# An edge tile, four and four PSUM banks, a shifted weight plan, and a weight decoding that VectorE shares with ScalarE and GpSimd

## The chip, the cores and the metric

One Trainium2 chip, one core. The time is that of the program on the device in microseconds; lower is better. The profile is that of one execution of its own.

## What is computed

Linear attention, then a mixture of four experts weighted by given probabilities, then a feed-forward layer with a sigmoid GELU:

```python
# q, k, v: (4, 8, 576, 64)
q_s = softmax(q, axis=-1); k_s = softmax(k, axis=2)
x = einsum('bhsd,bhde->bhse', q_s, einsum('bhsd,bhse->bhde', k_s, v))
x = x.transpose(0, 2, 1, 3).reshape(2304, 512)
p = domain_probs / domain_probs.sum(-1)                       # (2304, 4)
out = sum(p[:, e:e+1] * (relu(x @ w1[e]) @ w2[e]) for e in range(4))   # w1 (4, 512, 1024)
h = out @ w_in                                                # (512, 2048)
return (h * sigmoid(1.702 * h)) @ w_out                       # (2048, 512)
```

`w_in` and `w_out` come as float64, that is as pairs of 32-bit words; everything else is float32.

## The kernel before

Every float32 matrix is split into a high and a low part (`h`, `l`), each of a type that TensorE reads in one pass, and a product is three matmuls (high-high, high-low, low-high). The first layer of each of the two networks is done as a 2x2 block product with seven products in place of eight (Strassen's form, as Winograd ordered it): the weights give seven blocks (`a11, a12, a22, s1..s4`), the tokens seven "forms" (`b11, b21, b22, t1..t4`). One product is six matmuls (L836).

Work goes in units: a unit is 256 columns of the hidden width, 16 for the experts and 8 for the feed-forward layer. Tokens are in three groups of 2x512, 2x256 and 2x384 columns (groups 0, 1, 2). Pass 0 of each network runs all units over group 0; pass 1 runs all units over groups 1 and 2, one step each. A step (`step`) has five stages, in an order written out by hand (STAGES): products m1 to m7 into the PSUM tiles `px`, `py`, `pz`; ScalarE copies (`p1c`, `u2c`, `u3c`) and VectorE additions (`p1a`, `u2a`, `u3a`, L866) that combine them; ScalarE's relu or GELU into `h_hi` (`ra` to `rd`, L879) and VectorE's `h_lo` (`la` to `ld`, L885, L889). A step finishes the one before it (a dash marks its operations). TILES and REST, in stages 4 and 1, are the second layer: for every 128 tokens six matmuls of 512 columns into a PSUM tile `po` (L952), which VectorE adds to the accumulator `acc` (L964 for the experts, L973 for the feed-forward layer).

PSUM has eight banks: the pool `psc` has five (tag "c": `px`, `py`, `pz`), the pool `pso` three (tag "o": `po`, and the attention's transposes and products `pm`, `pb`, `pk`, `t`, `px` of L531). A tile takes the bank of its pool that has been free longest, and its first writer waits for that bank's last reader.

At the end of each stage `prepare` makes the next unit's weight parts by the plans TWO (two steps a unit) or ONE (pass 0): sums on GpSimd (L762), the high part on ScalarE (L768), the low part on GpSimd (L774). Then the background is pumped: `pump` advances generators, `pumps[0]` times a stage on average. They are the attention of the later batches in the first half of pass 0 (rate 2), and in pass 1 of the experts `decode_all` (rate 1.4), which turns 32 tiles of 128x512 float64 weights into float32. A tile takes four pumps there (`decode`): lines 803 and 804; 808 and 811; 815 and 818; 820 and 823. Only line 823 is GpSimd's, the others VectorE's. The load of the next tile (`w64`, line 796, two buffers) is issued on SP's queue after a tile's third pump, and the store of its result (line 824) after the second pump of the next tile. Each engine works through its instructions in the order of the program.

The forms of groups 0 and 2 lie in the pools `xp0` and `xq0`, opened from the right-hand end of SBUF (4 KB a tile and partition, the last ending 32 bytes short of the end); those of group 1 lie in `xp1`, on the left.

Of the kernel before, what the change touches and what calls it, by code (L numbers as in the profile page):

```python
# [8 lines left out]
F32 = mybir.dt.float32  # L9
# [6 lines left out]
ALU = mybir.AluOpType  # L16
# [6 lines left out]
def tile_linear_attention_moe_gelu(  # L23
# [56 lines left out]
    evp = ctx.enter_context(tc.tile_pool(name="evp", bufs=7))  # L80
    xop = ctx.enter_context(tc.tile_pool(name="xop", bufs=2))
    dram = ctx.enter_context(tc.tile_pool(name="dram", bufs=1, space=DRAM))
    psc = ctx.enter_context(tc.tile_pool(name="psc", bufs=5, space=PSUM))
    pso = ctx.enter_context(tc.tile_pool(name="pso", bufs=3, space=PSUM))

    ident = const.tile([P, P], F32, name="ident")
    ones = const.tile([P, SP], F32, name="ones")
# [10 lines left out]
    def open_pool(name, **kw):  # L98
        pools[name] = tc.tile_pool(name=name, reuse_waits="tile", **kw)
        pools[name, "p"] = pools[name].__enter__()  # L100

    def close_pool(name):
        pools.pop(name).__exit__(None, None, None)
        pools.pop((name, "p"))

    wi32 = dram.tile([DM, FF], F32, name="wi32")
    wo32 = dram.tile([FF, DM], F32, name="wo32")

# [19 lines left out]
    def probs_ops():  # L128

        y = {}

        def pr_(_):
            n = evp.tile([SP, B, NCH, E], F32, tag="ev", name="prn")
            sh = evp.tile([SP, 3 * SP], F32, tag="ev", name="shift")
            sm = evp.tile([SP, B * NCH], F32, tag="ev", name="prs")
            y.update(sh=sh, sm=sm, f=n.rearrange("p b c e -> p (b c) e"))  # L140
            S_.dma_start(
                out=n.rearrange("p b c e -> p b (c e)"),
                in_=probs.rearrange("(b p c) e -> p b (c e)", b=B, c=NCH),
            )
# [12 lines left out]
        def pp(_):  # L157
            f, sh = y["f"], y["sh"]
            ps = y["ps"] = pso.tile([P, NT // P, E], F32, tag="o", name="pr_ps")
            by_tile = ps.rearrange("p (x t) e -> p x t e", t=3)  # L160
            by_group = f.rearrange("p (x g) e -> p x g e", g=4)
            for t in range(3):
                first = [(0, *divmod(t * P, SP))]
                first += [((g * SP) - t * P, g, 0) for g in range(4) if t * P < g * SP < (t + 1) * P]
                for x, (o, g, p0) in enumerate(first):
                    T.matmul(
                        by_tile[:, :, t, :], sh[:, SP + p0 - o : SP + p0 - o + P], by_group[:, :, g, :],
                        start=(x == 0), stop=(x == len(first) - 1), skip_group_check=True,
                    )

        def pc(_):
            V.tensor_copy(pr, y["ps"])

        return {"pr": pr_, "pn": pn, "pp": pp, "pc": pc}


# [39 lines left out]
    def attend(b, j, pool, bufs, x, small_bufs):  # L216
# [10 lines left out]

        def bank(s, n):
            if n in KBANK[b]:
                return psc.tile(s, F32, tag="c", name=f"{n}_{nm}")  # L230
            return pso.tile(s, F32, tag="o", name=f"{n}_{nm}")

        def qm(_):
            y["qm"] = small([SP, 2 * NCH], "qm")
# [171 lines left out]
    def attend2(b, j, c0, nc_, keys, live):  # L406
# [9 lines left out]
            return pools["attn2", "p"].tile(s, F32, tag=tag or n, bufs=BUFS.get(tag or n, 2), name=f"{n}{nm}")  # L416

        def bk(n, s):
            return pso.tile(s, F32, tag="o", name=f"{n}_{nm}")

        def lq(_):
            y["q"] = t_("q", [SP, 2, nc_, D])
# [226 lines left out]
    def to_x2(i, ti, lt):  # L649

        src = acc[ti]

        def go():
            pt = pso.tile([P, KT, P], F32, tag="o", name=f"pt{ti}")
            for kk in range(KT):
                T.transpose(pt[:, kk, :], src[:, kk * P : (kk + 1) * P], ident)
            o = xop.tile([P, KT * P], F32, tag="xo", name=f"xt{ti}")
            copy(V if stage[1] else A, o, pt.rearrange("p k t -> p (k t)"))
            A.dma_start(out=x_d["ffn", i][:, :, lt * P : (lt + 1) * P], in_=o.rearrange("p (k t) -> p k t", t=P))

        x2.append((stage[0], go))
# [130 lines left out]
    def decode(src, dst, pool, nm):  # L792

        n = src.shape[1]
        w = pool.tile([P, n], I64, tag="w64", name=f"w64{nm}")
        S_.dma_start(out=w, in_=src)
        yield
        w = w.bitcast(I32).rearrange("p (n t) -> p n t", t=2)
        top, low = w[:, :, 1], w[:, :, 0].bitcast(U32)
        s = pool.tile([P, n], I32, tag="ds", name=f"ds{nm}")  # L800
        t = pool.tile([P, n], I32, tag="dt", name=f"dt{nm}")
        o = pool.tile([P, n], F32, tag="do", name=f"do{nm}")
        V.tensor_scalar(out=s, in0=top, scalar1=0x7FF00000, scalar2=None, op0=ALU.bitwise_and)
        V.tensor_scalar(
            out=s, in0=s, scalar1=float(1151 << 20), scalar2=float(896 << 20), op0=ALU.min, op1=ALU.max
        )
        yield
        V.tensor_scalar(
            out=s, in0=s, scalar1=float(896 << 20), scalar2=8.0, op0=ALU.subtract, op1=ALU.mult
        )  # L810
        V.scalar_tensor_tensor(  # L811
            out=s, in0=top, scalar=-(1 << 31), in1=s, op0=ALU.bitwise_and, op1=ALU.bitwise_or
        )
        yield
        V.tensor_scalar(
            out=t, in0=top, scalar1=3, scalar2=0x007FFFF8, op0=ALU.logical_shift_left, op1=ALU.bitwise_and
        )
        V.tensor_tensor(out=t, in0=t, in1=s, op=ALU.bitwise_or)
        yield
        V.scalar_tensor_tensor(  # L820
            out=o, in0=low, scalar=2.0**-52, in1=s.bitcast(F32), op0=ALU.mult, op1=ALU.mult
        )
        G.tensor_tensor(out=o, in0=o, in1=t.bitcast(F32), op=ALU.add)  # L823
        late.append(lambda: S_.dma_start(out=dst, in_=o))
        yield
# [16 lines left out]
    def mm1(g, i, m, ho):  # L842
# [7 lines left out]
        def product(ps, w, t, first):  # L850
            def go(_):
                if first:
                    y[ps] = psc.tile([P, n], F32, tag="c", name=f"{ps}{nm}")
                mm(y[ps], W1[m, w], X[i, t], first, True)

            return go
# [36 lines left out]
        if m < NPLAIN:  # L893
            def half(x, ft, kh):
                def go(_):
                    if kh == 0:
                        y["c" + x] = psc.tile([P, n], F32, tag="c", name=f"c{x}{nm}")
                    b = f"b{kh + 1}{1 + (i == 'R')}"
                    mm(y["c" + x], W1[m, f"a{ft + 1}{kh + 1}"], X[0, b], kh == 0, kh == 1)

                return go

            tile_of = {"a": (0, 0, "ca"), "c": (1, 0, "cc")}
            for x, (ft, *_) in tile_of.items():
# [31 lines left out]
    def mm2(g, i, lt, m, ho):  # L936
# [6 lines left out]
        y = {}  # L943

        def product(_=None):
            y["ps"] = ps = pso.tile([P, DM], F32, tag="o", name=f"po{g}_{ti}")
            n = 0
            for ft in range(FT):
                hh, hl = h_hi[:, ft, s], h_lo[:, ft, s]
                wh, wl = W2[m, ft]  # L950
                for a, b in ((hh, wh), (hh, wl), (hl, wh)):
                    T.matmul(ps, a, b, start=(n == 0), stop=(n == 3 * FT - 1))  # L952
                    n += 1
# [49 lines left out]
        (("s1",), ("a11", "s2"), ("a12",), ("+s2", "s3"), ("s4",)),  # L1003
        ((), ("+s1",), ("+s3",), ("a22",), ("+s4",)),
    )
    ONE = ((("s1", "a11"), ("s2", "a12"), ("+s2", "s3"), ("+s1", "s4", "+s3"), ("a22", "+s4")),)

    def prepare(m, names):
        for x in names:
# [57 lines left out]
    def step(k_, tiles, before):  # L1067
# [77 lines left out]
        a1:s5 c1:s5 St3:b0@V Ht3:b0 y0:s4 a2:s5 ha22:6 la22:6@G y1:s4 z0:s4 ra:s5 Lt3:b0@V la:s5 z1:s4 c2:s5 rc:s5  # L1145
        lc:s5 y2:s4 ha12:6 hs2:6 la12:6@V y3:s4 z2:s4 hs3:6 ls2:6@V z3:s4 ls3:6@V hs1:6 ls1:6@G St4:b0@G
    """
    open_pool("xp0", bufs=2, side="right")
    open_pool("x0", bufs=1)
    open_pool("attn", bufs=1)  # L1150
# [3 lines left out]
    V.memset(warm, 0.0)  # L1154
    small0 = attn.tile([P, 1], F32, name="small0")
    V.memset(small0, 0.0)
    hot = psc.tile([P, P], F32, tag="c", name="hot")

    def keep_warm(n):

# [42 lines left out]
    for x in START.split():  # L1203
# [20 lines left out]
    for layer, g0 in (("moe", LM), ("ffn", 2 * LM + LF)):  # L1224
        ka, kb = at_step[g0 - 4, 0], at_step[g0 - 1, 0]
        if layer == "moe":
            when(ka, 3, drain, lambda: open_pool("xp1", bufs=2))
        when(ka, 3, load_now(layer, 1))
        when(ka, 4, forms_now(layer, 1, OWN))
        when(kb - 1, 4, load_now(layer, 2))  # L1230
        when(kb, 1, forms_now(layer, 2, SHARED, work(1.4, decode_all(tiles)) if layer == "moe" else lambda: None))
    kc = at_step[2 * LM - 1, 2]
    when(kc - 1, 0, drain, load_now("ffn", 0))
    when(kc, 1, forms_now("ffn", 0, SHARED))
# [4 lines left out]
    for y in tiles_at(len(steps) - 1):  # L1239
        for x in mm2(*y):  # L1240
            x()
    for name in ("xp1", "xq0", "xp0"):
        close_pool(name)
    manual.__exit__(None, None, None)

# [25 lines left out]
```

## Time and profile before

| | us |
|---|---|
| median of 3 runs | 1256.05 (1254.97 to 1257.68) |
| profiled execution | 1257.08 |
| its span | 1255.3 |
| TensorE busy | 1217.9 (97%) |
| VectorE busy | 848.0 (68%) |
| ScalarE busy | 464.6 (37%) |
| GpSimd busy | 356.8 (28%) |

The share of busy time is a mean over stretches with different limits. TensorE's matmuls overlap in the records, so that its pace is read from pieces of the chain (so many matmuls in so many us), not from the duration of one. VectorE's instructions overlap by some 0.08 us at their ends. Times in the rows are us from the start of the span.

### The profile page before, as it was taken

Reading aid. Unit: us, or ns where it says so; the run is one execution under the profiler, and the core shown is the slowest. Engines: PE = TensorE matmul, PEld = TensorE weight load, DVE = VectorE, ACT = ScalarE, POOL = GpSimd, SP = SyncE. Lnnn points to the kernel's source line nnn. Section 1 sums busy time; section 2 is a strip of 40 time slices with the busy share of each in tenths; the row PEclk is TensorE's granted clock in tenths of the full one; section 3 lists DMA queues with packets and bytes.
Section 4 is the critical chain, followed back from the end, with each engine's and each line's share of the span. In section 5 each row is a group of like instructions: output and inputs, shape, how many; then the busy total and the mean of one; then the engine's idle time right before and its main releaser. Section 6 shows DMA issues by size and latency. Waiting matters only on the chain.

```text
span 1255.3 us, 17519 instructions
## 1 busy us (share of the span) xinstructions
PE 1217.9 (97%) x6276; PEld 1047.6 (83%) x6276; DVE 848.0 (68%) x1416; ACT 464.6 (37%) x1010; POOL 356.8 (28%) x389
## 2 busy tenths in 40 slices
PE   8999899999999999999999999999999999999998
PEld 8777678777887898888989899998787778999997
DVE  7865777666567758999999855577446665455454
ACT  6534344433434351222222222145645444333332
POOL 5425657454553001111211311025555400000000
PEclk9999899999999999999999999999999999999999
DMA  9875965754566375766556332535664655333333
GB/s 211 261 267 179 313 179 199 215 206 143 203 226 201 110 214 189 213 214 219 202 201 227 129 105 77 191 120 195 225 231 180 206 170 161 109 96 115 117 94 84
DMA packets 134423, 225.86 MB, mean 180 GB/s; under 512 B 30400, under 2 KB 62144, under 8 KB 133696
## 3 DMA queue, kind: packets, MB, share of 16 engines
q1 hardware_dynamic: 124832, 220.02, 54.3%
q10 hardware_dynamic: 9504, 4.72, 1.3%
q8 instruction: 50, 0.82, 0.3%
q14 instruction: 37, 0.30, 0.1%
HBM read 137.40 MB, written 87.29 MB: 179 GB/s over the span
## 4 chain that ended last, share of the span: by engine, by line
PE 71%; DVE 18%; DMA 5%; issue 3%; ACT 2%; POOL 1%; SPq 0%; ACTq 0%; DVEq 0%; POOLq 0%
PE po L952 35%; PE px L836 17%; PE pz L836 7%; PE py L836 5%; DVE acc L964 4%; DVE h_lo L885 3%; DMA w64o<-in_moe_w_out 1%; DMA w64i<-in_moe_w_in 1%; DVE u L866 1%; PE p L378 1%; PE pk L506 1%; DMA k_a<-a 1%; DMA q<-in_q 1%; PE px L358 1%; DVE dso L811 1%
## 5 line engine op out<-in xcount | busy, mean ns | idle before, releaser
L952 PE MATMUL po<-w,h_hi 128*128 128x512 f32 x1728 | 541.7, 395 | 14.2 <-DVE acc L964 8.0
L952 PEld LDWEIGHTS po<-w,h_hi 128*128 128x128 f32 x1728 | 320.8, 189 | 82.3 <-DVE acc L964 9.5
L952 PE MATMUL po<-w,h_lo 128*128 128x512 f32 x864 | 339.3, 393 | 5.2 <-DVE h_lo L885 5.2
L964 DVE SCALAR_TENSOR_TENSOR acc<-po,pr,acc 128x512 f32<-128x512 f32 x270 | 195.2, 746 | 77.6 <-PE po L952 77.3
L952 PEld LDWEIGHTS po<-w,h_lo 128*128 128x128 f32 x864 | 163.3, 189 | 42.3 <-DVE h_lo L885 7.0
L110 ACT COPY u<-px 128x384 f32<-128x384 f32 (+2 forms) x138 | 65.2, 472 | 243.5 <-PE px L836 240.1
L973 DVE TENSOR_TENSOR acc<-po,acc 128x512 f32<-128x512 f32 x126 | 85.9, 689 | 62.2 <-PE po L952 62.0
L774 POOL TENSOR_TENSOR s<-s,s 128x256 fp32r<-128x256 f32 x94 | 77.1, 821 | 140.3 <-ACT s L768 121.1
L866 DVE TENSOR_TENSOR u<-pz,u 128x384 f32<-128x384 f32 (+2 forms) x138 | 75.5, 547 | 58.0 <-ACT u L110 57.3
L787 POOL TENSOR_TENSOR w<-rc,w 128x512 fp32r<-128x512 f32 x46 | 59.8, 1299 | 75.6 <-ACT w L781 56.2
L879 ACT ACTIVATE h_hi<-px 128x256 fp32r<-128x256 f32 (+2 forms) x45 | 21.8, 484 | 152.0 <-PE px L836 151.8
L885 DVE SCALAR_TENSOR_TENSOR h_lo<-u,h_hi 128x256 fp32r<-128x256 f32 (+2 forms) x90 | 62.9, 723 | 14.1 <-ACT h_hi L879 14.1
L774 POOL TENSOR_TENSOR a<-ra,a 128x256 fp32r<-128x256 f32 x69 | 52.1, 757 | 57.6 <-ACT a L768 56.6
L823 POOL TENSOR_TENSOR doi<-doi,dti 128x512 f32<-128x512 f32 x16 | 21.1, 1320 | 155.7 <-DVE doi L820 149.2
L762 POOL TENSOR_TENSOR s<-ra 128x256 f32<-128x256 f32 x48 | 41.1, 857 | 84.2 <-DMA ra<-wi 54.2
L866 DVE TENSOR_TENSOR p<-py,p 128x384 f32<-128x384 f32 (+2 forms) x69 | 37.8, 548 | 37.3 <-PE py L836 32.9
L781 ACT CAST w<-rc 128x512 fp32r<-128x512 f32 x48 | 29.6, 620 | 70.5 <-PE po L952 69.8
L879 ACT ACTIVATE h_hi<-u 128x256 fp32r<-128x256 f32 (+2 forms) x90 | 46.3, 515 | 24.9 <-DVE u L866 24.9
L823 POOL TENSOR_TENSOR doo<-doo,dto 128x512 f32<-128x512 f32 x16 | 21.1, 1320 | 96.8 <-DVE doo L820 83.5
L110 ACT COPY p<-px 128x384 f32<-128x384 f32 (+2 forms) x69 | 32.8, 476 | 39.2 <-PE px L836 38.9
L885 DVE SCALAR_TENSOR_TENSOR h_lo<-px,h_hi 128x256 fp32r<-128x256 f32 (+2 forms) x45 | 24.6, 546 | 31.1 <-ACT h_hi L879 31.1
L768 ACT CAST s<-s 128x256 fp32r<-128x256 f32 x96 | 36.8, 401 | 20.6 <-POOL s L762 15.3
(312 smaller groups left out, 2458.8 us busy)
## 6 DMA issues: line engine op xcount, KB each, us to landing
w<-k_w SPq DMA_DIRECT2D x54, 512.0 KB, 4.5
k_w<-w SPq DMA_DIRECT2D x48, 512.0 KB, 4.9
a<-k_a SPq DMA_DIRECT2D x84, 256.0 KB, 2.8
k_s<-s SPq DMA_DIRECT2D x84, 256.0 KB, 4.5
s<-k_s SPq DMA_DIRECT2D x84, 256.0 KB, 3.3
k_a<-a SPq DMA_DIRECT2D x75, 256.0 KB, 4.9
ra<-in_moe_w SPq DMA_DIRECT2D x19, 512.0 KB, 4.4
rc<-in_moe_w SPq DMA_DIRECT2D x16, 512.0 KB, 5.9
```

Source lines behind the costliest of these rows:

```text
L110: (eng.copy if eng is A else eng.tensor_copy)(o, i)
L762: G.tensor_tensor(out=o, in0=block_w(m, l), in1=block_w(m, r), op=op)
L774: eng.tensor_tensor(out=lo, in0=block_w(m, x), in1=hi.bitcast(F32), op=ALU.subtract)
L787: eng.tensor_tensor(out=lo, in0=raw[m, 1][:, c, :], in1=hi.bitcast(F32), op=ALU.subtract)
L823: G.tensor_tensor(out=o, in0=o, in1=t.bitcast(F32), op=ALU.add)
L836: T.matmul(ps, a[:, kk, :], b[:, kk, :], start=(start and n == 0), stop=(stop and n == 5), skip_group_check=True,)
L866: return lambda _: V.tensor_tensor(out=y[o], in0=y[ps], in1=y[o], op=ALU.add)
L879: A.activation(hi, y[c], AF.Relu)
L885: V.scalar_tensor_tensor(out=lo, in0=y[c], scalar=0.0, in1=hi.bitcast(F32), op0=ALU.max, op1=ALU.subtract)
L952: T.matmul(ps, a, b, start=(n == 0), stop=(n == 3 * FT - 1))
L964: V.scalar_tensor_tensor(out=acc[ti], in0=ps, scalar=pe, in1=acc[ti], op0=ALU.mult, op1=ALU.add)
L973: V.tensor_tensor(out=acc[ti], in0=ps, in1=acc[ti], op=ALU.add)
```

## The change

Five edits:

- A tile of 224 bytes a partition (`edge`) is opened at the right-hand end of SBUF ahead of `xp0` and kept, so that every tile of `xp0` and `xq0` starts 224 bytes lower.
- After the start both PSUM pools are closed and opened again with four banks each.
- In the plan ONE, a12 is made one stage later, and so are the parts of s2 and s3.
- In `decode`, VectorE's steps of lines 808 and 820 go. ScalarE makes `s` (scale 8 and a bias) and, from the low word, `o` (scale 2^-52), both behind line 804; the sign is put in one pump later, in front of the "or" with the mantissa; GpSimd then multiplies `o` by `s` and adds `t`. A tile has four pumps as before.
- The background's rate while decoding is 1.25 and not 1.4.

```diff
+    open_pool("psc", bufs=5, space=PSUM)
+    open_pool("pso", bufs=3, space=PSUM)
...
         V.tensor_scalar(
             out=s, in0=s, scalar1=float(1151 << 20), scalar2=float(896 << 20), op0=ALU.min, op1=ALU.max
         )
-        yield
-        V.tensor_scalar(
-            out=s, in0=s, scalar1=float(896 << 20), scalar2=8.0, op0=ALU.subtract, op1=ALU.mult
-        )
-        V.scalar_tensor_tensor(
-            out=s, in0=top, scalar=-(1 << 31), in1=s, op0=ALU.bitwise_and, op1=ALU.bitwise_or
-        )
+        A.activation(s, s, AF.Copy, bias=-float(896 << 23), scale=8.0)
+        A.activation(o, low, AF.Copy, scale=2.0**-52)
         yield
         V.tensor_scalar(
             out=t, in0=top, scalar1=3, scalar2=0x007FFFF8, op0=ALU.logical_shift_left, op1=ALU.bitwise_and
         )
+        yield
+        V.scalar_tensor_tensor(
+            out=s, in0=top, scalar=-(1 << 31), in1=s, op0=ALU.bitwise_and, op1=ALU.bitwise_or
+        )
         V.tensor_tensor(out=t, in0=t, in1=s, op=ALU.bitwise_or)
         yield
-        V.scalar_tensor_tensor(
-            out=o, in0=low, scalar=2.0**-52, in1=s.bitcast(F32), op0=ALU.mult, op1=ALU.mult
-        )
+        G.tensor_tensor(out=o, in0=o, in1=s.bitcast(F32), op=ALU.mult)
         G.tensor_tensor(out=o, in0=o, in1=t.bitcast(F32), op=ALU.add)
...
-    ONE = ((("s1", "a11"), ("s2", "a12"), ("+s2", "s3"), ("+s1", "s4", "+s3"), ("a22", "+s4")),)
+    ONE = ((("s1", "a11"), ("s2",), ("a12", "s3"), ("+s2", "+s1", "s4"), ("+s3", "a22", "+s4")),)
...
+    open_pool("edge", bufs=1, side="right")
+    pools["edge", "p"].tile([P, 56], F32, name="edge")
     open_pool("xp0", bufs=2, side="right")
...
     load_w(NSTART + 1, 0)
+    close_pool("pso")
+    close_pool("psc")
+    open_pool("psc", bufs=4, space=PSUM)
+    open_pool("pso", bufs=4, space=PSUM)
...
-        when(kb, 1, forms_now(layer, 2, SHARED, work(1.4, decode_all(tiles)) if layer == "moe" else lambda: None))
+        when(kb, 1, forms_now(layer, 2, SHARED, work(1.25, decode_all(tiles)) if layer == "moe" else lambda: None))
```

## Rows read from the trace of the kernel before

**Rows 1.** Busy time by stretch: start:end, length, each engine's busy us, PEclk, DMA.
```profile
105.00:310.00 205.00, 191.14 (x898) 155.25 (x897) 142.41 (x216) 82.65 (x179) 119.24 (x134) 0.98 0.67 212
...
450.00:512.00 62.00, 60.04 (x326) 53.95 (x325) 48.91 (x95) 18.68 (x42) 9.23 (x7) 0.97 0.64 203
512.00:712.00 200.00, 194.21 (x1056) 173.35 (x1055) 193.28 (x353) 42.24 (x102) 38.08 (x31) 1.00 0.62 203
...
960.00:1040.00 80.00, 75.75 (x336) 61.44 (x335) 53.57 (x74) 36.68 (x70) 22.71 (x24) 0.98 0.53 172
```

**Rows 2.** The chain that ended last, in order of time: start us, length us, what.
```profile
575.86 1.98 DVE acc L964 x3
...
603.46 1.98 DVE acc L964 x3
...
718.17 1.77 PE px L836 x12
...
723.41 1.06 PE px L836 x6
...
744.33 1.77 PE px L836 x12
...
905.19 5.46 PE po L952 x24
910.65 2.80 PE px L836 x12
```

**Rows 3.** TensorE's waits in 105 to 310 us: us in total, times, longest.
```profile
PE po L952 <- DVE acc L964: 4.9, 3, 2.3
PE pb L491 <- ACT qT L527: 1.6, 3, 0.5
PE po L952 <- ACT qT L527: 1.3, 1, 1.3
```

**Rows 4.** TensorE's waits in 450 to 712 us.
```profile
PE po L952 <- DVE h_lo L885: 5.2, 4, 1.4
PE po L952 <- DVE acc L964: 2.5, 2, 2.0
```

**Rows 5.** TensorE's wait in 960 to 1040 us.
```profile
PE po L952 <- DVE acc L973: 4.2, 3, 2.5
```

**Rows 6.** VectorE's groups in 475 to 700 us: busy us, mean ns, idle before.
```profile
L964 DVE SCALAR_TENSOR_TENSOR acc<-po,pr,acc 128x512 f32<-128x512 f32 x82 | 56.8, 741 | 0.0
L804 DVE TENSOR_SCALAR dso<-dso 128x512 int32<-128x512 int32 x16 | 11.7, 733 | 0.5
L885 DVE SCALAR_TENSOR_TENSOR h_lo<-u,h_hi 128x256 fp32r<-128x256 f32 x16 | 10.4, 692 | 0.0
...
L820 DVE SCALAR_TENSOR_TENSOR doo<-w64o,dso 128x512 f32<-128x512 uint32 x15 | 10.2, 683 | 0.0
...
L808 DVE TENSOR_SCALAR dso<-dso 128x512 int32<-128x512 int32 x15 | 6.3, 420 | 0.2
```

**Rows 7.** Timeline while decoding: start us, length us, instruction, idle before it.
```profile
587.95 0.50 ACT L879 ACTIVATE h_hi<-px 128x384 fp32r<-128x384 f32 x1 [4.10 <-PE px L836]
587.97 1.36 POOL L823 TENSOR_TENSOR doo<-doo,dto 128x512 f32<-128x512 f32 x1 [6.33 <-DVE doo L820]
...
588.21 1.40 DVE L804 TENSOR_SCALAR dso<-dso 128x512 int32<-128x512 int32 x1
...
589.53 0.28 PE L836 MATMUL pz<-t1hmoe,s 128*128 128x256 f32 x1
...
589.53 0.41 DVE L866 TENSOR_TENSOR p<-py,p 128x256 f32<-128x256 f32 x1
...
592.84 0.50 PE L952 MATMUL po<-w,h_lo 128*128 128x512 f32 x1 [1.27 <-DVE h_lo L885]
```

**Rows 8.** A ScalarE copy of 128x512 from SBUF to SBUF (the page's costliest groups).
```profile
L781 ACT CAST w<-rc 128x512 fp32r<-128x512 f32 x48 | 29.6, 620 | 70.5 <-PE po L952 69.8
```

**Rows 9.** VectorE's waits in 450 to 712 us.
```profile
DVE dsi L803 <- DMA w64i<-in_moe_w_in: 6.2, 3, 3.8
```

More of the change, by code (lines that the diff above doesn't have):

```diff
@@ L82, in tile_linear_attention_moe_gelu @@
     dram = ctx.enter_context(tc.tile_pool(name="dram", bufs=1, space=DRAM))
-    psc = ctx.enter_context(tc.tile_pool(name="psc", bufs=5, space=PSUM))
-    pso = ctx.enter_context(tc.tile_pool(name="pso", bufs=3, space=PSUM))
     ident = const.tile([P, P], F32, name="ident")
@@ L158, in pp @@
             f, sh = y["f"], y["sh"]
-            ps = y["ps"] = pso.tile([P, NT // P, E], F32, tag="o", name="pr_ps")
+            ps = y["ps"] = pools["pso", "p"].tile([P, NT // P, E], F32, tag="o", name="pr_ps")
             by_tile = ps.rearrange("p (x t) e -> p x t e", t=3)
@@ L229, in bank @@
             if n in KBANK[b]:
-                return psc.tile(s, F32, tag="c", name=f"{n}_{nm}")
-            return pso.tile(s, F32, tag="o", name=f"{n}_{nm}")
+                return pools["psc", "p"].tile(s, F32, tag="c", name=f"{n}_{nm}")
+            return pools["pso", "p"].tile(s, F32, tag="o", name=f"{n}_{nm}")
         def qm(_):
@@ L418, in bk @@
         def bk(n, s):
-            return pso.tile(s, F32, tag="o", name=f"{n}_{nm}")
+            return pools["pso", "p"].tile(s, F32, tag="o", name=f"{n}_{nm}")
         def lq(_):
@@ L653, in go @@
         def go():
-            pt = pso.tile([P, KT, P], F32, tag="o", name=f"pt{ti}")
+            pt = pools["pso", "p"].tile([P, KT, P], F32, tag="o", name=f"pt{ti}")
             for kk in range(KT):
@@ L852, in go @@
                 if first:
-                    y[ps] = psc.tile([P, n], F32, tag="c", name=f"{ps}{nm}")
+                    y[ps] = pools["psc", "p"].tile([P, n], F32, tag="c", name=f"{ps}{nm}")
                 mm(y[ps], W1[m, w], X[i, t], first, True)
@@ L896, in go @@
                     if kh == 0:
-                        y["c" + x] = psc.tile([P, n], F32, tag="c", name=f"c{x}{nm}")
+                        y["c" + x] = pools["psc", "p"].tile([P, n], F32, tag="c", name=f"c{x}{nm}")
                     b = f"b{kh + 1}{1 + (i == 'R')}"
@@ L945, in product @@
         def product(_=None):
-            y["ps"] = ps = pso.tile([P, DM], F32, tag="o", name=f"po{g}_{ti}")
+            y["ps"] = ps = pools["pso", "p"].tile([P, DM], F32, tag="o", name=f"po{g}_{ti}")
             n = 0
@@ L1156, in tile_linear_attention_moe_gelu @@
     V.memset(small0, 0.0)
-    hot = psc.tile([P, P], F32, tag="c", name="hot")
+    hot = pools["psc", "p"].tile([P, P], F32, tag="c", name="hot")
     def keep_warm(n):
@@ L1241, in tile_linear_attention_moe_gelu @@
             x()
-    for name in ("xp1", "xq0", "xp0"):
+    for name in ("xp1", "xq0", "xp0", "edge", "pso", "psc"):
         close_pool(name)
```

## The prediction, made before the changed kernel ran

> **What bounds the kernel now.** I read the table of stretches first, then the chain that ended last in order of time, then who waited for whom, and last VectorE's lines and timeline. The stretches [rows 1] show TensorE busy almost throughout; what it loses lies in a few places: 105 to 310 us (attention of the later batches beside the experts), 450 to 712 us (the decoding of the FFN weights) and 960 to 1040 us (the forms of the next token group are made). VectorE is the thing to look at there: in 512 to 712 us it is busy 193.28 of 200 us, and no other engine but TensorE is near that (ScalarE 42.24, GpSimd 38.08).
>
> The chain [rows 2] gives TensorE's own pace: 24 second-layer matmuls of 512 columns in 5.46 us (0.2275 us each), 12 first-layer ones of 512 in 2.80 us (0.233), 6 of 384 in 1.06 us (0.177); the piece of 1.77 us holds six of 384 and six of 256, so 256 columns take 0.118. It gives the period too: one unit (a 256- and a 384-step of pass 1) takes 744.33 - 718.17 = 26.16 us without decoding, where the chain is all TensorE, and 603.46 - 575.86 = 27.60 us with it, where the chain goes through VectorE. So decoding costs about 1.4 us a unit. In 200 us there are 7.3 such units: 10.6 us lost by the period, 200 - 194.21 = 5.8 us by the idle time. I take 8. At 26.16 us a unit that work needs some 192 us.
>
> The waits name what ends last. In 105 to 310 us [rows 3] TensorE waits for a VectorE accumulation to leave one of the three "o" banks (4.9 us in 3 waits) and for ScalarE to empty such a bank (1.6 us in 3, and 1.3 in 1): 7.8 us that are bank waits. (A longer wait near 134 us is for data of the first attention head, and no edit touches it.) In 450 to 712 us [rows 4] it is 5.2 us for h_lo, which is data and waits because VectorE is late, and 2.5 us for banks. In 960 to 1040 us [rows 5] 4.2 us, banks again, in 3 waits. Two of these places are long enough that the granted clock fell: 0.97 over 62 us and 0.98 over 80 us [rows 1], which at half speed is 1.9 us and 1.6 us lost.
>
> **The change part by part.**
>
> *Four "o" banks in place of three.* A tile of the second layer is six matmuls, 6 x 0.2275 = 1.37 us [rows 2]; a fourth bank lets TensorE go on by that much before it must wait. 105 to 310 us: 3 x 1.37 = 4.1 of the 4.9 us, and the four shorter waits whole, 2.9: at most 7.0. Nothing if VectorE is only as late one tile further on; it is busy 142 of 205 us there, so it catches up, and I take 5. 450 to 512 us: between 0 and 4.4 us (2.5 of waits and 1.9 of clock); the longest wait, 2.0 us, exceeds one tile, so I take 2. 960 to 1040 us: the longest, 2.5 us, keeps 1.1, the others vanish: at most 3.1 and 1.6 us of clock; I take 3. Late next: VectorE itself.
>
> *Four "c" banks in place of five.* At most four are alive at once (the px and pz of the last step, px and py of this one). With no bank to spare, pz takes the bank that the VectorE addition of py has just left. In the step of [rows 7] that addition ran from 589.53 to 589.94 us and pz began at 589.53: TensorE would have waited 0.4 us. Going through all 69 such pairs, four lie so, all in the decoding, and the others have room. Cost 0 to 2 us; if VectorE stops being late it is near nothing, and I take 0.5.
>
> *VectorE's two steps leave.* Line 808 (0.420 us) and line 820 (0.683 us) [rows 6] go, 1.10 us for each of 32 tiles, 35 us in all. What is taken over lies beside: two ScalarE copies of a 128x512 tile, 0.62 us each by the nearest row [rows 8], 40 us on an engine that is a fifth busy; one more GpSimd product of 1.36 us [rows 7], 43 us on an engine equally idle. The pumping rate falls from 1.4 to 1.25 a stage, so each unit decodes 11% less and the decoding ends about one unit later, near 730 us, well ahead of its use.
>
> *What the GpSimd product costs VectorE.* In [rows 7] the sum of line 823 starts at 587.97, and line 804 on VectorE, which starts at 588.21, takes 1.40 us where an operation of its kind takes 0.42 [rows 6]: it was held for a microsecond. It is not always so: mean over least, summed over lines 803, 804 and 885 (six rows; two stand in [rows 6], 0.733 and 0.692 us where the least is about 0.42), is 18 us for 32 sums, 0.58 us each. Accumulations, which read PSUM, don't show it. The new product starts right behind the step that makes the sign, the sum follows it, and the decoding's next VectorE step is at least one stage off, so mostly the kernel's own operations meet them: I take 0.58 us for each of the 64 (bounds 0 and 1.36).
>
> VectorE's load in 512 to 712 us then: 193.3, less 25 tiles x 1.10 with overlaps (23.8), less 11% of the rest of the decoding (25 tiles x 2.7 us x 0.107 = 7.2), less the present holds (25 x 0.58 = 14.4) gives 147.9; 22.3 tiles with two holds each of 0.58 add 25.9: 174 us for TensorE's 192. VectorE is no longer the bound there, but at 90% it is still late now and then. I leave 3 of the 8 us in 7.3 units, 3.5 in the longer window: gain 4.5 (bounds 0 and 10.6).
>
> *What the copies put in ScalarE's way.* ScalarE works in order, and the first copy waits for line 804 on VectorE; behind it stand the activations that make h_hi. Where the pump falls at the end of stage 1, the chain after the last tile is an accumulation of 0.74 us [rows 6], lines 803 and 804 with 0.42 each, two copies of 0.62, an h_hi of 0.50 [rows 7] and an h_lo about as long: 3.8 us, while TensorE has four products in front of it, 3.5 us (twice the 1.77 us piece [rows 2]). It is just too long. One pump in five falls there: 6 tiles, 0 to 1 us each. I take 1.5.
>
> *The load of w64.* Line 803 already waits for its DMA (6.2 us in 3 waits [rows 9]), holding the queue behind it. The slower pump starts the load 1.6 stages ahead and not 1.4, but a punctual VectorE has less time to hide it; I count these as cancelling (bounds: 2 us either way).
>
> *The moved weight steps (ONE).* A12 goes one stage later, and so do the products of s2 and s3. Each part is used a stage or more after that, in the next step; the work is the same. 0, with 1 us either way.
>
> *The 224 bytes at the edge.* They move the forms of groups 0 and 2 to other addresses. Does an address set the pace? 0.233 against 0.2275 us at 512 columns might say so: 1026 matmuls (21 steps of 42 and 144 in the start) x 5.8 ns = 6 us, and perhaps 3 us at 384. But 256 columns, from a pool that is not at the end and does not move, lie on the same line as 384 and 512 (0.118, 0.177, 0.233: 0.057 per 128 columns). So the pace goes with the line and the width, and I take 0 (bounds 9 us either way).
>
> **Sum.** 5 + 2 + 3 + 4.5 - 0.5 - 1.5 = 12.5 us from the profiled execution's 1257.08: 1244.6. The median of the runs shown is 1.0 us below that execution, so I say **1244**.
>
> **The rivals.** *GpSimd holds VectorE for good (slower).* If each of the 64 operations holds it for its whole 1.36 us, VectorE's load is 147.9 + 22.3 x 2.72 = 209 us for TensorE's 192: at the 97% reached now, 215 us, 23 us too many, and 33 over the whole decoding (32 / 22.3 tiles) against 10 now. With the 8 us of banks elsewhere kept: +15, 1271. Slower begins where a hold exceeds 1.1 us. For it: the 1.40 us of line 804. Against it: the mean of 0.58, and accumulations that are not held. The Trainium skill, "SBUF — State Buffer", section "Who interferes with whom", has the rule behind it: a VectorE instruction with two SBUF inputs or in its two-port mode contends with a GpSimd one that reads SBUF, and the second to issue is blocked until the first ends. By that rule the trace agrees for each single collision, but not that every operation meets one.
>
> *Only the banks help.* VectorE, made faster, waits for w64 instead [rows 9], and h_lo is as late as now: no gain in 450 to 712 us, 8 - 2 = 6 us: 1250. For it: the load's lead is already used up.
>
> *The pace changes.* 9 us more are gained: 1235; or lost: 1253. Against it: the three widths on one line.
>
> *It does nothing.* TensorE is 97% busy, the waits may only change their names: 1256.
>
> **How the numbers follow.** Forecast 0.55 (its range 1238 to 1250); only the banks 0.15; a better pace 0.09; a worse one or nothing 0.11; GpSimd's hold 0.10. The range 1233 to 1258 leaves out most of the hold and the far end of a better pace, and takes in the bounds of the rest. A measurement of this kernel can tell about 0.2%, 2.5 us, from no change. Faster: 0.55 + 0.15 + 0.09 = 0.79; the same 0.10; slower 0.11.
>
> **What would show it.** In the changed profile: the bank waits of [rows 3] and [rows 5] at 2 us or less each, clock at 1.00 in 450 to 512 us; VectorE at about 90% in 512 to 712 us, the unit's period near 26.5 us, decoding until about 730 us; two ScalarE copies near 0.62 us and two GpSimd operations near 1.36 us a tile. Wrong it is if the period stays at 27 us with VectorE full (hold) or with VectorE waiting for w64 (load), if TensorE waits for h_hi behind the copies, if pz waits for its bank, or if 12 first-layer matmuls of 512 columns no longer take 2.80 us.

## The result and the profile after

The changed kernel takes **1237.35 us** (1235.35 to 1238.49) where the kernel before takes 1256.38 in the same comparison: the ratio is 0.9847, its 95% interval 0.9830 to 0.9864. The forecast was 1244, its range 1233 to 1258. The profiled execution took 1237.38 us with a span of 1235.6, 19.7 us less than that of before.

In the tables of stretches the columns are start:end, length, busy us of TensorE, its weight load, VectorE, ScalarE and GpSimd, then the granted clock, DMA share and GB/s. The kernel after, to be laid beside [rows 1] (712 to 850 us is new):

```profile
105.00:310.00 205.00, 198.57 (x939) 162.06 (x938) 147.89 (x222) 86.61 (x186) 121.58 (x136) 0.99 0.67 212
...
450.00:512.00 62.00, 61.72 (x341) 55.66 (x341) 50.29 (x89) 23.01 (x52) 21.83 (x16) 1.00 0.61 192
512.00:712.00 200.00, 194.99 (x1074) 174.72 (x1074) 171.75 (x293) 65.94 (x151) 79.79 (x57) 1.00 0.62 201
712.00:850.00 138.00, 135.48 (x731) 121.46 (x730) 90.57 (x140) 44.05 (x99) 29.37 (x32) 0.99 0.37 124
...
960.00:1040.00 80.00, 80.00 (x383) 67.58 (x382) 54.71 (x81) 38.22 (x75) 18.89 (x20) 1.00 0.63 201
```

The stretches of the bank waits gained: TensorE does 41 matmuls more in 105 to 310 us and 47 more in 960 to 1040, where it never waits. In 512 to 712 us VectorE has fallen from 193.28 to 171.75 us, and yet TensorE is idle for 5.0 us of 200, against 5.8 before; and in 712 to 850 us, where before it was busy throughout, 2.5 us are lost and the clock is 0.99. What TensorE waits for in the kernel after (us in total, times, longest), in 105 to 310 us (first two lines) and 512 to 740 us:

```profile
PE pb L491 <- DVE dg L487: 4.7, 1, 4.7
PE pk L506 <- DVE acc L961: 1.7, 1, 1.7
...
PE px L833 <- ACT u L110: 5.0, 6, 1.6
PE po L949 <- ACT h_hi L876: 2.5, 1, 2.5
```

The bank waits of [rows 3] and [rows 5] are gone but for one of 1.7 us; the first line is the wait for the first attention head's data, which no edit touches. In the decoding the wait for h_lo of [rows 4] has gone too, but seven waits for **ScalarE**, 7.5 us in all, stand in its place. The chain that ended last, in order of time (start us, length us, what), beside [rows 2]:

```profile
581.26 1.77 PE px L833 x12
...
607.28 1.77 PE px L833 x12
...
690.05 1.77 PE px L833 x12
...
712.00 1.25 DVE dso L803
713.27 0.44 DVE dso L804
...
714.97 0.39 ACT h_hi L876
715.39 5.42 PE po L949 x15
720.82 1.77 PE px L833 x12
...
746.79 1.77 PE px L833 x12
748.56 1.04 PE py L833 x6
...
772.76 1.77 PE px L833 x12
```

Two things are to be seen. A unit without decoding takes 772.76 - 746.79 = 25.97 us and not 26.16, and six matmuls of 384 columns take 1.04 us and not 1.06: the pace has changed. And at 715 us the chain goes through VectorE and ScalarE to a TensorE that stood still for 2.5 us; behind that the granted clock was at its lower level for a part of the next 15 second-layer matmuls, which took 5.42 us. In e4 (below), which has the same decoding and the same stop of 2.5 us, they took 3.83 us, and the clock in 712 to 850 us is 1.00:

```profile
714.07 3.83 PE po L949 x15
```

So the clock cost 1.6 us here beside the 2.5, and it doesn't fall behind that stop in every execution.

**Where the time went, step by step.** For the kernels below, the starts of the same matmul (the first of m2 in chosen steps, and the last matmul) were laid beside those of the kernel before, and the differences of neighbouring marks taken. Times of the heading are those of before; negative is gained, in us. "Banks", "edge", "decoding" name parts of the change.

| kernel | to 147 | 147-305 | 305-459 | 459-516 | 516-733 | 733-854 | 854-1023 | to the end | sum |
|---|---|---|---|---|---|---|---|---|---|
| after | -0.5 | -7.3 | -1.2 | -3.5 | **+2.1** | -0.9 | -7.4 | -1.4 | -19.9 |
| e1: banks alone | 0.3 | -7.8 | -1.1 | -3.5 | 0.5 | 0.0 | -7.6 | 0.0 | -19.3 |
| e2: decoding alone | 0.7 | 0.0 | 0.0 | -3.0 | **+5.0** | 0.0 | -1.6 | 0.0 | 1.0 |
| e3: after, no edge | -2.6 | -5.6 | -1.2 | -3.3 | 2.7 | 0.0 | -8.1 | 0.0 | -18.0 |
| e4: after, old ONE | -1.1 | -8.0 | -1.2 | -3.4 | 0.6 | -0.9 | -8.1 | -1.4 | -23.5 |
| e6: after, old decoding | -2.0 | -7.3 | -1.2 | -2.3 | 0.4 | -0.9 | -7.6 | -1.4 | -22.3 |
| e7: after, copies later | -0.5 | -5.7 | -1.2 | -4.1 | **-7.9** | -0.9 | -7.5 | -1.4 | -29.1 |
| e10: e7 and a tile in front | -3.3 | -6.2 | -2.7 | -3.9 | -5.8 | -0.3 | -8.8 | -0.6 | -31.7 |
| e11: e7's decoding alone | -2.1 | 0.0 | 0.0 | -3.8 | **-5.3** | 0.0 | -1.7 | 0.0 | -13.0 |

The first column varies by some 2 us between kernels that are alike up to there, so it says nothing. The others show the parts apart: banks in 147 to 459 and 854 to 1023 us, edge where nothing else happens (733 to 854 and the end), decoding in 516 to 733. The wait of 459 to 516 us goes with the banks or with the decoding, whichever is there. The columns hold some of the clock as well. In 854 to 1023 us e2 and e11 gain 1.6 and 1.7 us without the banks: they have the stop of 2.5 us of [rows 5], but in their profiles the clock doesn't fall behind it. The six matmuls after it in the chain of the kernel before, and in that of e2:

```profile
973.96 2.92 PE po L952 x6
```

```profile
976.45 1.66 PE po L949 x6
```

### The profile page after: what moved, and what is told of

Same layout as the page of the kernel before. It is cut to its first block, busy times and chain, and to the rows that moved or that the text cites. A ratio compares the mean times of both kernels' runs of the same rounds, so it can differ in the third digit from the quotient of the medians.

```text
span 1235.6 us, 17644 instructions
## 1 busy us (share of the span) xinstructions
PE 1210.8 (98%) x6276; PEld 1044.5 (85%) x6276; DVE 829.6 (67%) x1352; ACT 497.4 (40%) x1074; POOL 414.6 (34%) x421
## 4 chain that ended last, share of the span: by engine, by line
PE 82%; DVE 7%; DMA 5%; issue 3%; ACT 2%; SPq 1%; POOL 0%; ACTq 0%; DVEq 0%; POOLq 0%
PE po L949 42%; PE px L833 20%; PE pz L833 10%; PE py L833 5%; DVE h_lo L882 2%; DVE acc L961 1%; PE pk L506 1%; DMA w64i<-in_moe_w_in 1%; DMA q<-in_q 1%; PE px L531 1%; DMA k<-in_k 1%; PE hot L1161 1%; PE pt L656 1%; DMA rc<-in_moe_w 1%; DMA x_ffn<-xt 1%
## 5 line engine op out<-in xcount | busy, mean ns | idle before, releaser
L774 POOL TENSOR_TENSOR s<-s,s 128x256 fp32r<-128x256 f32 x94 | 79.7, 855 | 84.5 <-ACT s L768 72.1
L882 DVE SCALAR_TENSOR_TENSOR h_lo<-u,h_hi 128x256 fp32r<-128x256 f32 (+2 forms) x90 | 77.0, 874 | 22.8 <-ACT h_hi L876 22.6
L819 POOL TENSOR_TENSOR doi<-doi,dsi 128x512 f32<-128x512 f32 x16 | 27.9, 1747 | 134.9 <-DVE dsi L814 58.6
L819 POOL TENSOR_TENSOR doo<-doo,dso 128x512 f32<-128x512 f32 x16 | 27.2, 1703 | 65.4 <-issue 32.9
```

What stands on the lines that cost most here:

```text
L774: eng.tensor_tensor(out=lo, in0=block_w(m, x), in1=hi.bitcast(F32), op=ALU.subtract)
L819: G.tensor_tensor(out=o, in0=o, in1=s.bitcast(F32), op=ALU.mult)
L882: V.scalar_tensor_tensor(out=lo, in0=y[c], scalar=0.0, in1=hi.bitcast(F32), op0=ALU.max, op1=ALU.subtract)
```

## The experiments

| kernel | median us (range) | ratio to before, 95% |
|---|---|---|
| e1 banks alone | 1238.15 (1236.93 to 1238.68) | 0.9867 (0.9840 to 0.9893) |
| e2 decoding alone | 1258.81 (1258.12 to 1260.95) | 1.0031 (1.0020 to 1.0042) |
| e3 after, no edge | 1239.47 (1239.11 to 1241.34) | 0.9881 (0.9858 to 0.9904) |
| e4 after, old ONE | 1236.43 (1233.55 to 1237.41) | 0.9842 (0.9826 to 0.9857) |
| e6 after, old decoding | 1235.42 (1234.79 to 1239.18) | 0.9852 (0.9826 to 0.9878) |
| e7 after, copies later | 1228.09 (1227.74 to 1229.35) | 0.9781 (0.9766 to 0.9795) |
| e8 after, product on VectorE | 1239.88 (1238.69 to 1241.54) | 0.9877 (0.9861 to 0.9894) |
| e9 edge of 32 bytes | 1239.52 (1236.71 to 1241.83) | 0.9869 (0.9850 to 0.9888) |
| e9 edge of 64 bytes | 1239.92 (one run) | |
| e10 e7 and a tile in front | 1224.50 (1223.30 to 1225.94) | 0.9753 (0.9740 to 0.9766) |
| e11 e7's decoding alone | 1247.80 (1244.16 to 1250.92) | 0.9939 (0.9918 to 0.9959) |
| e12 e10 without the edge | 1227.44 (1225.88 to 1228.80) | 0.9779 (0.9763 to 0.9795) |

### The banks alone (e1)

```diff
     load_w(NSTART + 1, 0)
+    close_pool("pso")
+    close_pool("psc")
+    open_pool("psc", bufs=4, space=PSUM)
+    open_pool("pso", bufs=4, space=PSUM)
```

> The kernel before with one edit: from the end of the start on, four c banks and four o banks in place of five and three. Theory (the banks carry what was gained in 105 to 310 and 960 to 1040 us, some 14 us by the time of each step before against after): 1240 to 1244 us, TensorE's waits for an o bank gone in both stretches, the pace of 384 columns still 0.177 us. Rival (the decoding carries the gain, as the sum of the prediction had a third of it): 1246 to 1250. Rival (a c bank is missed): 1250 or more, with TensorE waiting in front of pz.

1238.15 us, below the range of the theory: the banks alone bring nearly all of the gain. (What the closing and opening of the pools does by itself no run tells.) The other side of the exchange shows as well. TensorE's waits in 512 to 740 us:

```profile
PE po L952 <- DVE h_lo L885: 3.1, 5, 0.7
PE pz L836 <- DVE p L866: 2.3, 4, 0.7
```

Four times pz waits for the VectorE addition that empties its bank: the price of the lost "c" bank while VectorE is late, as was worked out from the pairs. With the new decoding it vanishes (the waits of the kernel after have no such line).

Why the fourth "o" bank did more than its 1.37 us a wait is to be seen at the longest wait of [rows 5]. The timeline of the kernel before (start us, length us, instruction, idle time before it), and under it VectorE's of the kernel after at the same work:

```profile
973.23 1.87 DVE L973 TENSOR_TENSOR acc<-po,acc 128x512 f32<-128x512 f32 x3
...
973.96 1.22 PE L952 MATMUL po<-w,h_hi 128*128 128x512 f32 x2 [2.51 <-DVE acc L973]
...
976.92 0.69 DVE L973 TENSOR_TENSOR acc<-po,acc 128x512 f32<-128x512 f32 x1 [1.82 <-PE po L952]
```

```profile
961.23 2.47 DVE L970 TENSOR_TENSOR acc<-po,acc 128x512 f32<-128x512 f32 x4
```

VectorE is late by the same amount in both. But in pass 0, where these stretches lie, the second layer comes in **groups of four** tiles, and between two groups stand first-layer products, 4.2 or 5.6 us of them. With three banks the fourth tile of a group must wait for the first one's accumulation; six of the eleven waits over 0.25 us at the first matmul of a tile, the longest of [rows 3] (2.3 us) and of [rows 5] (2.5 us) among them, are at a fourth tile. With four banks each tile of a group has its own, and a late VectorE has until the next group. (In pass 1 a group has two or three tiles; the wait of 2.0 us at 488.77 us, the longest of [rows 4], is at the first tile of a group.) The kernel after's chain runs on without a piece between them:

```profile
955.33 5.46 PE po L949 x24
960.80 2.80 PE px L833 x12
```

### The decoding alone (e2), and all but the decoding (e6)

e2 is the kernel before with the diff's edit of `decode` and the rate 1.25; e6 is the kernel after with both taken back.

> The kernel before with the new decoding alone (two ScalarE copies, the GpSimd product, the pumping rate 1.25); banks, plan and edge as before. Theory: what VectorE wins, ScalarE gives back, because its copies wait for VectorE in front of the activations that make u and h_hi: 1251 to 1257 us, and TensorE waits for ScalarE (u, h_hi) in 512 to 720 us, some 5 us in all. Rival (decoding nets what the prediction gave it, 3 to 5 us or more): 1248 to 1252 with few such waits.

> The kernel after with the decoding of before (no copies, no GpSimd product, rate 1.4); banks, plan and edge stay. Theory (the new decoding nets nearly nothing): 1236 to 1240 us; VectorE back at 96% or more in 512 to 712 us, a unit there 27 us or more, but no stall behind ScalarE. Rival (decoding carries 4.5 us as in the prediction's sum): 1241 to 1244.

e2 is 3.7 us slower than before, more than its theory had it, and e6 1.9 us faster than after: the new decoding, as it stands, **costs** time. (The intervals of e6 and after overlap; that of e2 lies wholly above 1.) The first two lines of TensorE's waits of e2 in 512 to 740 us are those of the kernel after, with five "c" banks and three "o" banks, so that the four banks are not their cause; the other two are in front of `po` too, and the kernel after hasn't got them:

```profile
PE px L833 <- ACT u L110: 4.4, 6, 1.4
PE po L949 <- ACT h_hi L876: 1.9, 1, 1.9
PE po L949 <- DVE acc L961: 1.4, 1, 1.4
PE po L949 <- ACT dso L807: 1.1, 1, 1.1
```

### The copies one pump later (e7)

```diff
-        A.activation(s, s, AF.Copy, bias=-float(896 << 23), scale=8.0)
-        A.activation(o, low, AF.Copy, scale=2.0**-52)
         yield
         V.tensor_scalar(
             out=t, in0=top, scalar1=3, scalar2=0x007FFFF8, op0=ALU.logical_shift_left, op1=ALU.bitwise_and
         )
+        A.activation(s, s, AF.Copy, bias=-float(896 << 23), scale=8.0)
+        A.activation(o, low, AF.Copy, scale=2.0**-52)
         yield
```

> The kernel after, with the two ScalarE copies issued one pump later (behind the VectorE step that makes t), when the VectorE step that they need is long done. Same work on every engine. Theory (the copies stand at the head of ScalarE's queue waiting for VectorE, and u and h_hi behind them are late): TensorE's waits for u (5.0 us in 512 to 712 us) and for h_hi (2.5 us and some 1.8 us of clock near 715 us) go, 1229 to 1233 us. Rival (VectorE, held by GpSimd, is late anyway; the copies only name the wait): 1235 to 1238, the waits go to h_lo or u all the same.

1228.09 us, 9.3 us below the kernel after, with the same instructions on each engine. First the block as the kernel after has it (timeline):

```profile
645.90 1.74 POOL L819 TENSOR_TENSOR doo<-doo,dso 128x512 f32<-128x512 f32 x1 [5.48 <-ACT h_hi L876]
646.41 2.95 DVE L882 SCALAR_TENSOR_TENSOR h_lo<-u,h_hi 128x256 fp32r<-128x256 f32 x2
647.72 1.35 POOL L820 TENSOR_TENSOR doo<-doo,dto 128x512 f32<-128x512 f32 x1
...
651.51 0.43 DVE L804 TENSOR_SCALAR dso<-dso 128x512 int32<-128x512 int32 x1
...
652.04 0.63 ACT L807 ACTIVATE dso<-dso 128x512 int32<-128x512 int32 x1 [6.34 <-DVE dso L804]
652.57 0.64 ACT L808 ACTIVATE doo<-w64o 128x512 f32<-128x512 uint32 x1
653.12 0.47 ACT L110 COPY u<-px 128x384 f32<-128x384 f32 x1
...
653.64 0.44 PE L833 MATMUL px<-t4hmoe,a 128*128 128x384 f32 x1 [1.26 <-ACT u L110]
```

GpSimd's two operations hold two h_lo of VectorE, which take 2.95 us in place of twice 0.42. So VectorE comes to line 804 late. ScalarE, which works in order, stands idle for 6.34 us in front of a copy that waits for line 804, and behind that copy stands `u3c`, whose product m5 had ended near 648.1 us. m6 writes on in the same px tile and waits for `u3c`. The pump that sets this is the one at the end of stage 4 (TILES), ahead of `u3c` in stage 0. ScalarE's groups in 475 to 700 us tell how much it is in all (busy us, mean ns, idle before it); the first two lines are of the kernel after, the next two of e7:

```profile
L807 ACT ACTIVATE dso<-dso 128x512 int32<-128x512 int32 x14 | 8.8, 632 | 65.0 <-DVE dso L804 65.0
L807 ACT ACTIVATE dsi<-dsi 128x512 int32<-128x512 int32 x12 | 7.6, 633 | 48.9 <-DVE dsi L804 48.9
```

```profile
L811 ACT ACTIVATE dso<-dso 128x512 int32<-128x512 int32 x14 | 8.9, 633 | 34.6 <-DVE dso L804 34.6
L811 ACT ACTIVATE dsi<-dsi 128x512 int32<-128x512 int32 x12 | 7.6, 632 | 20.2 <-DVE dsi L804 20.2
```

113.9 us of idle time in front of 26 copies become 54.8, and what is left no longer keeps TensorE waiting. The stretch of 512 to 712 us of e7, and its only wait in 512 to 740:

```profile
512.00:712.00 200.00, 199.20 (x1102) 179.94 (x1101) 177.76 (x302) 71.79 (x161) 83.33 (x60) 1.00 0.63 207
```

```profile
PE po L949 <- DVE h_lo L882: 0.7, 1, 0.7
```

VectorE and GpSimd do more in the stretch than in the kernel after, since it runs faster, and TensorE waits no more. So the rival (VectorE is late anyway, the copies only pass it on) falls: VectorE's lateness hurt because it was handed on through ScalarE's queue.

### The late copies without the banks (e11)

> The kernel before with the new decoding alone, its copies issued one pump later; banks, plan and edge as before. Theory (with the copies out of ScalarE's way VectorE's relief is worth some 7 us by itself, as it was on top of the banks, and part of it because the o banks are emptied in time): 1246 to 1250 us, TensorE hardly waiting in 450 to 740 us; the bank waits of 105 to 310 and 960 to 1040 us stay. Rival (the relief pays only where four o banks stand behind it): 1252 to 1256.

1247.80 us, 7.3 us below the kernel before; e7 is 7.3 us below e6. By the steps from 459 to 733 us it is 9.1 and 10.1 us. So VectorE's relief is worth some 7 to 10 us with three "o" banks and with four, and it doesn't need the banks. That the medians agree to the tenth is chance (e11's four runs lie between 1244.16 and 1250.92), and what is gained isn't the same: e11 gains 3.8 us in 459 to 516 us, where e6 has most of it from the banks, and in 516 to 733 us 5.3 against 8.3, with one wait of 1.4 us in front of a `po` that e7 hasn't got. The waits of [rows 3] and [rows 5] stay as they were (po for acc: 4.9 us in 105 to 310, 4.3 in 960 to 1040).

### The product back on VectorE (e8)

```diff
-        G.tensor_tensor(out=o, in0=o, in1=s.bitcast(F32), op=ALU.mult)
+        V.tensor_tensor(out=o, in0=o, in1=s.bitcast(F32), op=ALU.mult)
```

> The kernel after with the decoding's product back on VectorE (as a tensor_tensor of 128x512), so one GpSimd operation a tile is left and the copies stay on ScalarE. Theory (a hold of some 0.55 us by the GpSimd product costs VectorE about what the product itself does, 0.68 us): VectorE's load in 512 to 712 us within 3 us of the 171.8 of the kernel after, the waits for u and h_hi stay, 1236 to 1239 us. Rival (the holds make VectorE late, and the copies only pass it on): load below 166 us, waits for u mostly gone, 1231 to 1234.

```profile
512.00:712.00 200.00, 195.86 (x1074) 174.30 (x1073) 175.27 (x313) 65.34 (x150) 38.91 (x33) 1.00 0.62 202
```

In the same 1074 matmuls GpSimd has 24 operations less than in the kernel after, and VectorE 22 products more (its lines in this stretch):

```profile
L819 DVE TENSOR_TENSOR doo<-doo,dso 128x512 f32<-128x512 f32 x14 | 9.6, 683 | 0.0
...
L819 DVE TENSOR_TENSOR doi<-doi,dsi 128x512 f32<-128x512 f32 x8 | 5.5, 683 | 0.0
```

They are 15.0 us, yet VectorE's load rises by 3.5 us only. So one GpSimd product had held VectorE for some (15.0 - 3.5) / 22 = **0.52 us**. Over the whole execution, where 32 products of 0.683 us raise VectorE's busy time from 829.6 to 836.4 us, it is 0.47; and as VectorE's instructions overlap at their ends, that counts too much: e8's busy time without the products is 819.6 us, which leaves 0.31. The product is near to neutral in either place; the waits for ScalarE stay (2.9 us for u, 3.6 for h_hi), as the theory said, though load and time lie a little above its ranges. The 2.5 us by which e8 is slower (intervals overlapping by a hair) lie mostly in a longer stop for h_hi near 715 us.

### The weight plan (e4), the edge (e3, e9)

```diff
-    ONE = ((("s1", "a11"), ("s2",), ("a12", "s3"), ("+s2", "+s1", "s4"), ("+s3", "a22", "+s4")),)
+    ONE = ((("s1", "a11"), ("s2", "a12"), ("+s2", "s3"), ("+s1", "s4", "+s3"), ("a22", "+s4")),)
```

> The kernel after with the weight steps of the one-step units (ONE) where they were before. Theory (they have a stage of room at either place): 1236 to 1239 us, and the time of each step within 1 us of the kernel after throughout. Rival (the moved steps take load out of crowded stages in 850 to 1020 us and are part of the gain there): 1239 to 1242, lost between 850 and 1020 us and in 105 to 430 us.

1236.43 us, overlapping with the kernel after. By steps it is behind nowhere: 854 to 1023 us -8.1 against -7.4, 147 to 459 us -9.2 against -8.5. The plan does nothing that these runs can tell.

e3:

```diff
-    open_pool("edge", bufs=1, side="right")
-    pools["edge", "p"].tile([P, 56], F32, name="edge")
```

> The kernel after without the 224 bytes at the edge. Theory (the address of the forms sets the pace of the 384-column matmuls, 0.177 against 0.173 us): 1241 to 1242 us, with 384 columns back at 0.177 us. Rival (address does nothing; the four banks changed the pace): 1236 to 1238.5 and 0.173 us.

1239.47 us: the edge is worth 2.1 us by the medians, and by the steps 0.9 + 1.4 us in pass 1 outside the decoding and 0.8 within it; pass 1 is where 384 columns run. e3 and e1 have 1.06 us for six matmuls of 384 columns as the kernel before, after and e6 1.04.

The two of e9 (the second with 16 in place of 8):

```diff
-    pools["edge", "p"].tile([P, 56], F32, name="edge")
+    pools["edge", "p"].tile([P, 8], F32, name="edge")
```

> The kernel after with 32 bytes at the edge in place of 224: the forms of groups 0 and 2 then start at multiples of 64 bytes (192 of 256) as with 224 bytes (0 of 256), and not at 32 of 64 as in the kernel before. Theory (a start on a multiple of 64 bytes is what quickens the 384-column matmuls): 0.174 us at 384 columns as in the kernel after, 1236 to 1239 us. Rival (a multiple of 256 bytes, or the distance from the end of the memory, is what counts): 0.177 us and 1238.5 to 1241.

> The kernel after with 64 bytes at the edge in place of 224: the forms of groups 0 and 2 then start at 160 of 256 bytes, which is 32 of 64 as in the kernel before. Theory (a start on a multiple of 64 bytes quickens the 384-column matmuls): 0.177 us at 384 columns, as in the kernel before. Rival (to be off the edge of the memory by any amount is enough): 0.174 us.

With 32 bytes six matmuls of 384 columns take 1.04 us, with 64 bytes 1.05, between the two. So neither "multiples of 64 bytes" (which wanted 1.06) nor "off the edge" (1.04) holds as it was put. By the steps both gain 0.5 + 0.8 us in 733 to 854 us and at the end, where the kernel after gains 0.9 + 1.4; the times of whole runs are too few and too wide apart to tell.

### A tile in front as well (e10), or alone (e12)

```diff
+    lead = ctx.enter_context(tc.tile_pool(name="lead", bufs=1))
+    lead.tile([P, 56], F32, name="lead")
     const = ctx.enter_context(tc.tile_pool(name="const", bufs=1))
```

e10 is e7 with this; every tile on the left, the stationary operands among them, moves up by 224 bytes. e12 is e10 without the edge.

> The kernel with the late copies, and 224 more bytes in front of the first pool, so that every operand of the experts' matmuls starts at a multiple of 256 bytes (before: all at 32 of 64; in the kernel after: only the moving forms of groups 0 and 2 at 0 of 256). Theory (a start address quickens only what it quickened in the kernel after, 384 columns): 1226.5 to 1229.5 us, second-layer matmuls still 0.2275 us. Rival (every width gains where its start is moved, by 1.6% as at 384 columns, so 2592 second-layer matmuls by up to 3.6 ns and the 256-column ones by 1.9): 1217 to 1225. Rival (the weights' new start costs): over 1230.

> The kernel with the late copies and with the 224 bytes in front of the first pool, but without those at the edge: stationary operands and W2 start at multiples of 256 bytes, the moving forms of groups 0 and 2 at 224 of 256 as in the kernel before. It fills the fourth field of a table of two by two (stationary start, moving start). Theory (the 512-column first-layer matmuls gain by the stationary start, the 384-column ones by the moving start): 12 first-layer matmuls of 512 columns in 2.72 us, 6 of 384 in 1.06 us, 1226 to 1229 us. Rival (both operands must be moved together for the 512-column gain): 2.80 and 1.06 us, 1230 to 1233 us.

The chain of e10 at pass 0 of the feed-forward layer, and that of e12:

```profile
923.08 5.44 PE po L951 x24
928.51 2.72 PE px L835 x12
```

```profile
754.80 1.04 PE px L835 x6
...
909.96 2.80 PE px L835 x12
```

In e10 twelve first-layer matmuls of 512 columns take 2.72 us, 0.2267 each, where all other kernels have 2.79 to 2.81: the pace of the second layer is had in the first. It gains 3.6 us on e7 by the medians (the two intervals meet at 0.9766), a time within the rival's range. The steps of the profiled executions show less: e10 is 2.8 us ahead before 147 us, where the table says nothing; what 512 columns gain behind that (3.3 us in 147 to 459 and 854 to 1023 us) is given back, 2.3 us in 459 to 733 us, with a wait of 1.5 us for u that e7 hasn't got, and 1.4 in the rest of pass 1. In its mechanism the result is neither expectation: the width that the kernel after had quickened, 384, gained no more, 512 gained 2.9%, 256 nothing. And e12 has the paces of the kernel after, 1.04 and 2.80, though each of its operands starts 224 bytes above where it starts in the kernel after: both its theory and its rival expected 1.06. What e12 and the kernel after share is the **distance** between the tiles on the left (weights) and those on the right (forms), 224 bytes less than before. By this distance: 0 (before, e1, e3): 1.06 and 2.80 us; 32 bytes: 1.04 and 2.81; 64: 1.05 and 2.79; 224 (after and e12): 1.04 and 2.80; 448 (e10): 1.04 and 2.72. That the distance counts rests on one pair of kernels; why, and what the best one is, stays open.

## Why the prediction was right, and where it was wrong

The time was within the stated range and on the right side, just below the 1238 to 1250 us of the forecast itself. But three terms were wrong, and that it came so near is in part luck: the banks gained 9.4 us more than was taken, and the decoding lost 4.6 us of that again.

| term | taken | bounds | measured (steps) |
|---|---|---|---|
| banks, 105 to 450 us | -5 | 0 to -7.0 | -8.5 |
| banks, 450 to 512 us | -2 | 0 to -4.4 | -3.5 |
| banks, 850 to 1040 us | -3 | to -4.7 | -7.4 |
| decoding with its copies and the "c" banks | -2.5 | -10.6 to +8 | +2.1 |
| edge | 0 | 9 either way | -2.2 |

**The banks** were under-rated, out of the bounds, by one step: "a fourth bank lets TensorE go on by that much before it must wait", that is by one tile, 1.37 us. The longest of the waits were at the fourth tile of a group of four, and what comes behind it is 4.2 us or more of other work; so a fourth bank ends such a wait whole, however long up to there. All the waits named in [rows 3] went, one of 1.7 us came, and 8.5 us were gained from 147 to 459 us. In 960 to 1040 us the 4.2 us of [rows 5] went with the clock's 1.6, and at 868 to 886 us two more waits, 1.0 us, which the prediction hadn't named:

```profile
PE pt L656 <- DVE xt L110: 0.7, 1, 0.7
PE po L952 <- DVE xt L110: 0.3, 1, 0.3
```

The clock's part is of the execution: it didn't fall behind the same stop in e2 and e11.

**VectorE's relief** was under-rated, **ScalarE's copies** were under-rated more. The relief was taken at 4.5 us; by e6 to e7 and before to e11 it is 7.3 by the medians. The copies were taken at 1.5 (0 to 6): by e7 they cost 9.3, of which 7.5 are the waits and 1.6 the clock after the stop at 715 us. The mechanism was named, ScalarE in order behind line 804, but only one of the pumps was costed, the end of stage 1 with h_hi behind it. There it came once and not in small pieces: the 2.5 us at 715 us. The other 5.0 us came at pumps that the sum left out: three waits of m6, 3.4 us, behind `u3c` after the pump of stage 4, and three of m5, 1.6 us, behind `u2c` after the pump of stage 2.

**GpSimd's hold** was taken at 0.58 us and is 0.3 to 0.5 (e8); the rival that it holds VectorE for good falls. VectorE was at 86%, not 90%. The product itself took longer than the 1.36 us taken from the sum, 1.74 us in the mean, as it is held too: it starts beside VectorE's "or" with the mantissa (line 817), and the one time that this had ended (720.83 us) it took 1.30. The Trainium skill, "SBUF — State Buffer", section "Who interferes with whom", says of such a pair that the second to issue is blocked until the first has ended; the rows at 646 us agree (0.42 us become about 1.5 each), and 0.3 to 0.5 is a mean over operations that met something and those that didn't.

**The "c" banks** came out nearly as worked out: four pairs, 2.3 us in e1 while VectorE is late (bound 2), nothing when it isn't. The load of w64 and the plan ONE did nothing visible; VectorE waits for w64 2.9 us in 450 to 712 us, where before it was 8.0 (the 6.2 of [rows 9], and 1.8 for the tiles of `w_out`).

**The edge** was taken at 0 because 256, 384 and 512 columns lie on one line. That was no evidence: three widths on one line can all be slow alike, and in the runs 384 columns left the line by themselves (the kernel after), and 512 after them (e10). The first thought, that 0.233 against 0.2275 us at 512 columns might be a matter of addresses, was right in the end (e10), though the edit of this change doesn't reach it.

Of the signs named ahead: the bank waits are at 2 us or less, the clock in 450 to 512 us is 1.00, the copies take 0.63 and 0.65 us, the decoding ended at 723.5 us. One of the signs of error came up, that TensorE waits for h_hi behind the copies. The unit's period of 26.5 us is not there as such: in the chain shown above units are clean (581.26 to 607.28 us, 26.0) or hit (690.05 to 720.82, 30.8). In the last line of the chances two are exchanged: a worse pace or nothing had 0.11 and GpSimd's hold 0.10, and the line gives 0.10 for the same and 0.11 for slower.

**The version that beats both** is e10: 1224.50 us, 0.9753 of before. It is the kernel after with the copies one pump later and a tile of 224 bytes in front. Of its lead over e7 the steps leave open how much comes from the tile.

## What to carry to other kernels

Count a buffer in the unit in which the work comes: if tiles come in groups of four with other work between the groups, a fourth buffer is worth up to the whole pause, and not one tile. An operation that is moved to an idle engine brings its wait with it: put it into that engine's order only where its input is already done, one pump later if need be, since everything behind it waits too. And before a part is called idle, ask whose queue it stands in, not how busy its engine is: ScalarE was a third busy and cost 9 us.

## What the runs showed of the hardware that was not expected

- The pace of a matmul on this chip depends on where its operands lie. 384 columns took 0.177 us each (six in 1.06) or 0.173 (1.04), 512 columns 0.2333 (twelve in 2.80) or 0.2267 (2.72), with the same instructions, by moving tiles by 224 bytes. Moving the forms down and moving the weights up by as much gave the same paces.
- A stop of 2.5 us in front of a TensorE that had been busy was followed by a fall of the clock to its lower level in some executions and not in others. In the kernel after, 15 matmuls took 5.42 us behind it (the chain at 715.39 us), in e4 3.83; in the kernel before, six took 2.92 us (at 973.96 us), in e2 1.66. So the clock cost 1.3 to 1.6 us beside the stop, where it fell.
